# Pooled attention and a Mish feed-forward on one core: keys, queries and values laid out by the host, with a new order of work

## Chip, cores, metric

One core of a Trainium2 chip. The metric is the device time of one execution in microseconds (us). TensorE is PE (its weight loads PEld), VectorE DVE, ScalarE ACT, GpSimd POOL; SyncE (SP) issues the DMAs.

## What is computed

The reference, cut to what matters (B, H, S, D = 4, 8, 1152, 64; float32):

```
q_pool = q.reshape(B, H, S // 2, 2, D).mean(axis=3)
scores = q_pool @ k.T / sqrt(D);  scores -= scores.max(-1)
attn = exp(scores);  attn /= attn.sum(-1) + 1e-9
x = (attn @ v) as 2304 tokens of 512
h = x @ w_in;  g = h * tanh(softplus(h));  out = g @ w_out        # 512 -> 2048 -> 512
```

## The kernel before

**Attention** runs in 32 steps i. A pair p = i // 2 is two heads of one batch; a step is one half (288) of the pair's 576 pooled queries. The 1152 keys are nine chunks c of 128. Scores have keys on the partitions, and the two heads side by side (128 x 2 x 288). The functions of a step, with engine:

- QK(i, c) (L200, PE) writes the scores of one chunk to PSUM; two buffers of it exist (pool psS). CP(i, c) (L215, ACT) copies them into T3, which has one half for even and one for odd steps; MX(i, c) (L218, DVE) folds them into a running maximum rmax, in place.
- MT (L228, PE) transposes rmax, TMAX (L235, DVE) reduces it, MB and MBb (L240, L247, PE) spread the maxima again into PSUM.
- SUB(i, g) (L253, DVE) subtracts them from one of four groups of chunks (2, 2, 2 and 3), in place in T3; EXP(i, g) (L258, ACT) follows.
- ADD(i, 0 to 4) (L262, POOL) sums the exponentials over the chunks into acc, of which one buffer exists. PV(i, c) (L272, PE) multiplies them with the values, PVE (L286, ACT) takes the product out of PSUM.
- FIN0 (L293, PE) sums acc over the partitions; FLN, FEX (ACT), FE (DVE), FU (POOL) and FX (DVE, L332) divide and write the columns of xT.

**Queries and keys** come as they lie in memory. For each pair, load_q (L90) and load_k (L99) issue two DMAs each and load_v (L113) one; QP (L122, POOL, DVE for pair 0) adds neighbouring queries; TG(p, 0 to 3) (L139, PE) makes nine 128 x 128 transposes of keys and six 96 x 96 of queries in PSUM, and TGc (L153, ACT) copies them in five pieces to kT and qT. For pair 0, first() (L164) does this ahead of everything, behind 52 idle transposes (L174) on PE.

**The order** is written out by hand: STEP gives each function of a step a due time for even and for odd steps, in units of one step from the step's own start, PAIR those of a pair (unit: one step, pair p counted from 2p), CONV0 those of the first weights' conversion, XE and XL those of the split of the first columns of xT. All entries are sorted by due time and issued so; every engine, and the DMA queue of SP, then works in that order.

**Feed-forward.** Weights and x are split in a high and a low fp32r part; conv(n, 0 to 5) (L437) splits the weights (piece n: ACT, three operations on DVE, ACT, POOL), split_h, split_l and split_x split xT. H_ (L500) and O_ (L533) make three products each on PE, in five blocks of the 2048 features over nine groups of 256 tokens. The first blocks begin while step 31 ends; the entries of the list END set that seam.

Of the kernel before, what the change touches and what calls it, by code (L numbers as in the profile page):

```python
# [22 lines left out]
def tile_pooled_attention_then_mish_ffn(ctx: ExitStack, tc: tile.TileContext, q, k, v, moe_w_in, moe_w_out, out):  # L23
    nc = tc.nc
    B, H, S, D = q.shape
# [41 lines left out]
    if True:  # L67
# [30 lines left out]

        def load_k(p):  # L99
            if p >= B * NP:  # L100
                return
            b, hp = divmod(p, NP)
            kn = pre.tile([P, NC, 2, D], F32, tag="kn", name=f"kn{p}")
            for j in range(2):
                o = kn[:, :, j] if p else T3[:, 1, j].rearrange("p a b -> p (a b)").rearrange("p (c d) -> p c d", d=D)
                sp.dma_start(out=o, in_=k[b, 2 * hp + j].rearrange("(p c) d -> p c d", c=NC))
                if p == 0:
                    (act.copy if j else dve.tensor_copy)(kn[:, :, j], o)
            raw[p][0] = kn
# [3 lines left out]
        def load_v(p):  # L113
            if p >= B * NP:
                return
            b, hp = divmod(p, NP)
# [1 line left out]
            sp.dma_start(out=vs[p], in_=v[b, 2 * hp:2 * hp + 2].rearrange("h (p c) d -> p h c d", c=NC))

        prepped = {}  # L120

        def QP(p):  # L122

            x = raw[p][1].rearrange("p j n m -> p n j m")
            qp = pre.tile([QB, 6, 2, D], F32, tag="qp", name=f"qp{p}")
            (pool if p else dve).tensor_tensor(qp, x[:, :, :, 0:D], x[:, :, :, D:2 * D], ALU.add)
            prepped[p] = qp.rearrange("p n j d -> p n (j d)")
# [8 lines left out]
        def kblock(p, c):
            return raw[p][0][:, c].rearrange("p j d -> p (j d)")

        def TG(p, g):  # L139

            if p not in qk:
                qk_tiles(p)
            x = ps1.tile([P, 512], F32, tag="x", name=f"xt{p}_{g}")
            a = 0
            for n in {0: range(0, 4), 1: range(4, 8), 2: (8,), 3: ()}[g]:
                pe.transpose(x[:, a:a + P], kblock(p, n), ident)
                a += P
            for n in {2: range(0, 3), 3: range(3, 6)}.get(g, ()):
                pe.transpose(x[:, a:a + QB], prepped[p][:, n], ident[0:QB, 0:QB])
                a += QB  # L150
            xt[p, g] = x

        def TGc(p, g):  # L153
            kT, qT = qk[p]
            x = xt.pop((p, g))
            if g < 2:
                act.copy(kT[:, 4 * g:4 * g + 4], x.rearrange("p (n m) -> p n m", m=P))
            elif g == 2:
                act.copy(kT[:, 8], x[:, 0:P])
                act.copy(qT[:, 0:HQ], x[:, P:P + HQ])  # L160
            else:
                act.copy(qT[:, HQ:SQ], x[:, 0:HQ])

        def first():  # L164

            load_q(0)
            load_k(0)
            load_w(0)
            load_w(1)
            QP(0)  # L170
# [4 lines left out]
            qk_tiles(0)  # L175
            kT, qT = qk[0]
            t = psS.tile([P, 2, 512], F32, tag="S", name="xq0")
            for n in range(6):
                pe.transpose(t[:, n // 3, n % 3 * QB:(n % 3 + 1) * QB], prepped[0][:, n], ident[0:QB, 0:QB])
            act.copy(qT[:, 0:HQ], t[:, 0, 0:HQ])  # L180
            dve.tensor_copy(qT[:, HQ:SQ], t[:, 1, 0:HQ])
            x = psS.tile([P, 8, P], F32, tag="S", name="xk0")
            for n in range(8):
                pe.transpose(x[:, n], kblock(0, n), ident)
            act.copy(kT[:, 0:4], x[:, 0:4])
            dve.tensor_copy(kT[:, 4:8], x[:, 4:8])
            x = ps1.tile([P, 512], F32, tag="x", name="xk0_2")
            pe.transpose(x[:, 0:P], kblock(0, 8), ident)
            act.copy(kT[:, 8], x[:, 0:P])
            load_q(1)  # L190
            load_k(1)
# [147 lines left out]
        LQ, LK = -3.4, -2.2  # L339
        STEP = [  # L340
            (QK, 0, -0.5640, -0.5584),
            (CP, 0, -0.4042, -0.4268),
            (QK, 1, -0.3837, -0.4118),
            (QK, 2, -0.3395, -0.3676),
            (MX, 1, -0.3197, -0.2976),
            (MX, 2, -0.2628, -0.2408),
            (CP, 1, -0.2498, -0.3491),
            (CP, 2, -0.2033, -0.1585),
            (QK, 3, -0.1849, -0.2352),
            (QK, 4, -0.1407, -0.1056),  # L350
            (MX, 3, -0.1181, -0.1833),
            (MX, 4, -0.0612, -0.0387),
            (CP, 3, -0.0587, -0.1195),
            (QK, 5, 0.0172, -0.0614),
            (CP, 4, 0.0823, 0.0864),
            (MX, 5, 0.0835, 0.1060),
            (CP, 5, 0.1429, 0.1655),
            (QK, 6, 0.1527, 0.1835),
            (QK, 7, 0.1969, 0.2277),
            (MX, 6, 0.2282, 0.2507),  # L360
            (MX, 7, 0.2850, 0.3076),
            (CP, 6, 0.2876, 0.3102),
            (CP, 7, 0.3445, 0.3722),
            (QK, 8, 0.3974, 0.3918),
# [9 lines left out]
            (SUB, 2, 1.1559, 1.1334),
            (EXP, 1, 1.2264, 1.2039),
            (PV, 0, 1.3117, 1.2407),
            (ADD, 0, 1.3313, 1.3504),
            (PV, 2, 1.3481, 1.4854),
            (SUB, 3, 1.3575, 1.3349),
            (EXP, 2, 1.4746, 1.4124),  # L380
            (PV, 1, 1.4797, 1.3173),
            (PV, 3, 1.5200, 1.3537),
            (ADD, 1, 1.5913, 1.6104),
            (EXP, 3, 1.6349, 1.6900),
            (PV, 5, 1.7675, 2.1034),
            (ADD, 2, 1.7928, 1.8231),
            (PV, 8, 1.9331, 2.1397),
            (PV, 4, 1.9734, 1.8085),
            (ADD, 3, 1.9942, 2.0245),
            (PV, 7, 2.0687, 2.0670),  # L390
            (ADD, 4, 2.1024, 2.1328),
            (PV, 6, 2.1090, 2.0267),
            (PVE, 2.1820, 2.2046),
            (FIN0, 2.2809, 2.2714),
            (FLN, 2.3836, 2.4113),
            (FEX, 2.4924, 2.4490),
            (FE, 2.5303, 2.5472),
# [3 lines left out]
        PAIR = [
            (QP, -1.7894),
            (TG, 1, -1.2869),
            (TGc, 1, -1.1948),
            (TG, 2, -1.1438),
            (TGc, 2, -1.0804),
            (TG, 0, -1.0176),
            (TGc, 0, -0.9498),
            (TG, 3, -0.0969),
            (TGc, 3, 0.0605),  # L410
# [217 lines left out]
        plan = []  # L628
        for fn, *a, t0, t1 in STEP:
            t = t0, t1  # L630
            for i in range(NS):
                if (i, fn) in GONE:
                    continue
# [65 lines left out]
```

## Time and profile before

| | us |
|---|---|
| median of 3 runs (879.56 to 880.87) | 880.58 |
| profiled execution, its own time | 881.09 |
| its span, first to last instruction | 878.9 |
| PE, DVE, ACT, POOL busy in the span | 856.1, 601.9, 536.2, 455.2 |

The mean granted clock of TensorE is 0.988 of full speed. Some 2.2 us of the execution's time lie outside the span. Busy times of PE hold waits inside a pipelined group of matmuls, so 97% of the span is not PE at its peak. A timeline row gives start, duration, engine, line, operation, output <- input, shape and count; in brackets the idle time ahead of it and who ended it. A row that merges two operations (x2) runs from the start of the first to the end of the second.

### The profile page before, as it was taken

The page shows a single profiled execution, that of the slowest core. Times are in us where ns is not written, and L with a number is a line of the kernel's source. Part 1 is how long each engine was busy: PE and PEld are TensorE (multiplying, and loading weights), DVE is VectorE, ACT ScalarE, POOL GpSimd, SP SyncE. Part 2 cuts the span into 40 slices and gives each one's busy share as a digit, 9 for nine tenths or more (in the row PEclk, how much of TensorE's full clock was granted, in tenths as well). Part 3 has the DMA queues.
Part 4 walks back from the last instruction along what each step waited for, and adds up shares of the span by engine and source line. Part 5 has one row for each costly group of instructions (what it writes and reads, how often), then busy time and mean ns, then how long its engine had stood idle before and what let it go on. Part 6 is the DMA issues. An engine that isn't in the chain of part 4 may idle for free. (4 is left out here: it accounts for less than half of the span.)

```text
span 878.9 us, 14807 instructions
## 1 busy us (share of the span) xinstructions
PE 856.1 (97%) x5668; PEld 601.2 (68%) x5668; DVE 601.9 (68%) x813; ACT 536.2 (61%) x995; POOL 455.2 (52%) x267
## 2 busy tenths in 40 slices
PE   6799999999999999999989999999999999999997
PEld 4455555555555555555547889999889999999996
DVE  5889999999999999999988743443545344422222
ACT  4688889888898888988875563333333333322221
POOL 1489899999999999999896510110111011100000
PEclk9699999999999999999999999999999999999999
DMA  6413233122332222320200220110221011001112
GB/s 180 131 29 81 55 82 81 38 72 58 79 82 49 61 70 66 81 55 29 76 1 3 71 72 25 48 48 25 73 70 51 25 49 49 25 15 42 41 48 72
DMA packets 75111, 50.76 MB, mean 58 GB/s; under 512 B 37409, under 2 KB 68641, under 8 KB 75041
## 3 DMA queue, kind: packets, MB, share of 16 engines
q1 hardware_dynamic: 75040, 49.82, 20.2%
q8 instruction: 45, 0.74, 0.3%
q14 instruction: 26, 0.20, 0.1%
HBM read 45.09 MB, written 4.72 MB: 57 GB/s over the span
## 5 line engine op out<-in xcount | busy, mean ns | idle before, releaser
L524 DVE TENSOR_TENSOR gl<-g,gh 128x256 fp32r<-128x256 f32 x144 | 65.3, 453 | 225.3 <-ACT gh L519 199.0
L216 ACT COPY T<-s 128x576 f32<-128x576 f32 x288 | 180.9, 641 | 52.2 <-DVE rmax L223 46.1
L514 ACT ACTIVATE g<-h 128x256 f32<-128x256 f32 x144 | 55.4, 385 | 245.3 <-PE h L509 245.3
L206 PE MATMUL s<-qT,kT 64*128 64x288 f32 x1152 | 195.8, 449 | 8.4 <-ACT T L216 7.2
L256 DVE TENSOR_TENSOR T<-T,Mb 128x1152 f32<-128x1152 f32 (+1 forms) x128 | 191.2, 1495 | 1.4 <-PE Mb L250 1.4
L465 POOL TENSOR_TENSOR wl<-wt,wh 128x512 fp32r<-128x512 f32 x32 | 42.2, 1318 | 263.8 <-ACT wh L462 219.9
L278 PE MATMUL pv<-T,vn 128*64 128x288 f32 x1152 | 175.0, 422 | 2.5 <-ACT pvs L289 2.5
L223 DVE TENSOR_TENSOR rmax<-s,rmax 128x576 f32<-128x576 f32 x224 | 168.9, 754 | 10.9 <-PE s L206 0.9
L268 POOL TENSOR_TENSOR acc<-acc,T 128x1152 f32<-128x1152 f32 x64 | 168.8, 2638 | 8.7 <-POOL acc L268 6.0
L260 ACT ACTIVATE T<-T 128x1152 f32<-128x1152 f32 (+1 forms) x128 | 164.5, 1285 | 7.2 <-DVE T L256 7.2
L509 PE MATMUL h<-xh,wh 128*128 128x256 f32 x576 | 162.1, 281 | 0.0
L509 PE MATMUL h<-xh,wl 128*128 128x256 f32 x576 | 161.8, 281 | 0.0
L509 PE MATMUL h<-xl,wh 128*128 128x256 f32 x576 | 161.6, 281 | 0.0
L206 PEld LDWEIGHTS s<-qT,kT 64*128 64x128 f32 x1152 | 90.4, 188 | 92.5 <-ACT T L216 74.7
L278 PEld LDWEIGHTS pv<-T,vn 128*64 128x64 f32 x1152 | 72.4, 137 | 71.4 <-issue 28.0
L509 PEld LDWEIGHTS h<-xh,wh 128*128 128x128 f32 x576 | 108.7, 189 | 8.2 <-issue 1.3
L509 PEld LDWEIGHTS h<-xl,wh 128*128 128x128 f32 x576 | 108.8, 189 | 6.0
L509 PEld LDWEIGHTS h<-xh,wl 128*128 128x128 f32 x576 | 109.2, 190 | 0.0
L266 POOL TENSOR_TENSOR acc<-T 128x1152 f32<-128x1152 f32 x32 | 84.7, 2648 | 32.0 <-PE Sb L300 13.8
L542 PE MATMUL o<-wh,gh 128*128 128x512 f32 x146 | 57.8, 396 | 1.0 <-ACT xT L554 1.0
L542 PE MATMUL o<-wl,gh 128*128 128x512 f32 x146 | 57.6, 394 | 0.0
L542 PE MATMUL o<-wh,gl 128*128 128x512 f32 x146 | 57.3, 392 | 0.0
(384 smaller groups left out, 1106.3 us busy)
## 6 DMA issues: line engine op xcount, KB each, us to landing
qn<-in_q_dram SPq DMA_DIRECT2D x32, 288.0 KB, 3.9
vn<-in_v_dram SPq DMA_DIRECT2D x16, 576.0 KB, 5.0
kn<-in_k_dram SPq DMA_DIRECT2D x30, 288.0 KB, 4.1
ri<-in_moe_w_in_dram SPq DMA_DIRECT2D x64, 128.0 KB, 2.2
ro<-in_moe_w_out_dram SPq DMA_DIRECT2D x16, 512.0 KB, 3.4
out_dram<-xT SPq DMA_DIRECT2D x18, 256.0 KB, 2.6
T<-in_k_dram SPq DMA_DIRECT2D x2, 288.0 KB, 5.0
```

The costliest lines, as they stand in the source:

```text
L206: pe.matmul(s[:, j, 0:HQ], kT[64 * j:64 * j + 64, c], qT[64 * j:64 * j + 64, hf * HQ:(hf + 1) * HQ], start=True, stop=True,)
L216: act.copy(T3[:, i % 2, c], ss[i, c])
L223: dve.tensor_tensor(r, ss[i, c], T3[:, i % 2, 0] if c == 1 else r, ALU.max)
L256: dve.tensor_tensor(x, x, Mbs[i][:, :, 0:HQ].unsqueeze(1).to_broadcast([P, w, 2, HQ]), ALU.subtract)
L260: act.activation(x, x, AF.Exp, scale=0.0625)
L266: pool.tensor_tensor(accs[i], t[:, 0:2], t[:, 2:4], ALU.add)
L268: pool.tensor_tensor(accs[i], accs[i], t[:, 2 * n + 2:2 * n + 4], ALU.add)
L278: pe.matmul(pvs[i][64 * j:64 * j + 64, 0:HQ], vn[:, j, c, :], T3[:, i % 2, c, j], start=(pvn[i] == 1), stop=(pvn[i] == NC),)
L509: pe.matmul(h[:, 0:UT], a, b, start=(m == 0), stop=(m == len(seq) - 1))
L514: act.activation(g, hs[bu, f], AF.Mish)
L524: dve.tensor_tensor(gl, ch.pop((bu, f)), f32(gs[bu, f][0]), ALU.subtract)
L542: pe.matmul(os_[bu][t], x, y, start=(first and m == 0), stop=(last and m == 2))
```

## The change

The host hands over q, k and v in other layouts: for each pair q as (head and feature 128, half 2, even or odd query 2, 288), k as (head and feature 128, chunk 9, 128), v as (128, head 2, chunk 9, 64). So kT is loaded by one DMA, QP adds straight into qT, and TG, TGc and the pair-0 transposes and copies are gone. All due times are new. A list FILL holds 281 entries with due times of their own for the first four steps or so; it has conv of the first four weight pieces and all early loads in it. Core of the diff:

```
-            qn = pre.tile([QB, 2, 6, P], F32, tag="qn", name=f"qn{p}")
-            for j in range(2):
-                sp.dma_start(out=qn[:, j], in_=q[b, 2 * hp + j].rearrange(...))
+            if p not in raw:
+                raw[p] = pre.tile([P, 2, 2, HQ], F32, tag="qn", name=f"qn{p}")
+            for a, z in halves or ((0, 2),):
+                sp.dma_start(out=raw[p][:, a:z], in_=q[p][:, a:z])
...
+            for a, z in parts or ((0, NC),):
+                sp.dma_start(out=qk[p][0][:, a:z], in_=k[p][:, a:z])
...
-        def TG(p, g):
-        def TGc(p, g):
...
+        def QP(p):
+            x = raw[p]
+            pool.tensor_tensor(qk[p][1], x[:, :, 0], x[:, :, 1], ALU.add)
+        def QH(n):
+            (pool if n in QHP else dve).tensor_tensor(qk[0][1][:, n], raw[0][:, n, 0], raw[0][:, n, 1], ALU.add)
...
         def first():
-            load_q(0)
...
+            qk_tiles(0)
             if NWARM:
...
-        LQ, LK = -3.4, -2.2
+        LQ, LK, QHP = -2.342, -2.2, (1,)
         STEP = [
...
-            (MX, 8, 0.4747, 0.4973),
-            (TMAX, 0.5963, 0.6255),
-            (SUB, 0, 0.8666, 0.7871),
-            (SUB, 1, 1.0113, 0.9887),
-            (FU, 2.5518, 2.5327),
-            (FX, 2.6512, 2.5981),
+            (MX, 8, 0.3645, 0.3594),
+            (TMAX, 0.6411, 0.6326),
+            (SUB, 0, 0.8146, 0.9207),
+            (SUB, 1, 1.0418, 0.7726),
+            (FU, 2.6678, 2.4802),
+            (FX, 2.9627, 2.7399),
...
-            (QP, -1.7894),
-            (TG, 1, -1.2869),
...
+            (QP, -0.8418),
...
+        FILL = [
+            (-0.700, load_q, 0, (0, 1)),
+            (-0.586, load_k, 0, (0, 2)),
+            (-0.536, load_k, 0, (2, 5)),
+            (-0.460, load_k, 0, (5, 9)),
+            (-0.429, QH, 0),
+            (-0.378, QK, 0, 0),
+            (-0.359, load_w, 0),
...
+            (1.536, conv, 1, 3),
+            (1.597, load_w, 3),
+            (1.798, load_q, 2),
...
-        XE = [5.349, 7.349, 9.349, ...
-        XL = 1.892
+        XE = [6.123, 8.123, 10.123, ...
+        XL = 0.055
...
-        for n, t in enumerate(CONV0):
-            plan += [(t[m], conv, n, m) for m in range(6)]
```

In the new order DVE does this in two steps of the steady part (steps in brackets, 0 being the even one; from the due times, not shown in the diff above): MX4[0] MX5[0] SUB2[-1] MX6[0] MX7[0] MX8[0] SUB3[-1] FE[-2] MX1[1] TMAX[0] MX2[1] MX3[1] SUB0[0] MX4[1] FX[-2] MX5[1] SUB1[0] MX6[1] MX7[1] SUB2[0] MX8[1] SUB3[0] FE[-1] MX1[2] TMAX[1] MX2[2] FX[-1] SUB1[1] MX3[2] SUB0[1].

## Rows read from the trace of the kernel before

**Rows 1.** Windows: stretch, us, busy PE, PEld, DVE, ACT, POOL (instructions), PE clock, DMA share, GB/s.
```profile
100.00:150.00 50.00, 50.00 (x351) 25.84 (x349) 47.32 (x56) 44.33 (x70) 46.64 (x26) 1.00 0.25 60
...
600.00:700.00 100.00, 100.00 (x643) 90.44 (x642) 47.91 (x87) 33.25 (x89) 12.69 (x10) 1.00 0.15 50
```

**Rows 2.** Timeline of DVE: TMAX of steps 4, 30 and 31.
```profile
85.70 0.83 DVE L237 TENSOR_REDUCE m<-mt 128x5 f32<-128x640 f32 x1 [0.43 <-PE mt L232]
...
439.73 0.83 DVE L237 TENSOR_REDUCE m<-mt 128x5 f32<-128x640 f32 x1 [0.43 <-PE mt L232]
...
453.71 0.82 DVE L237 TENSOR_REDUCE m<-mt 128x5 f32<-128x640 f32 x1
```

**Rows 3.** Timeline of DVE within one pair of steady steps.
```profile
212.14 1.61 DVE L223 TENSOR_TENSOR rmax<-s,rmax 128x576 f32<-128x576 f32 x2
213.67 1.34 DVE L256 TENSOR_TENSOR T<-T,Mb 128x1152 f32<-128x1152 f32 x1
214.94 0.75 DVE L223 TENSOR_TENSOR rmax<-s,rmax 128x576 f32<-128x576 f32 x1
215.60 1.34 DVE L256 TENSOR_TENSOR T<-T,Mb 128x1152 f32<-128x1152 f32 x1
...
218.40 1.95 DVE L256 TENSOR_TENSOR T<-T,Mb 128x1728 f32<-128x1728 f32 x1
220.26 0.75 DVE L223 TENSOR_TENSOR rmax<-s,rmax 128x576 f32<-128x576 f32 x1
...
221.87 0.83 DVE L237 TENSOR_REDUCE m<-mt 128x5 f32<-128x640 f32 x1 [0.43 <-PE mt L232]
222.61 0.45 DVE L334 SCALAR_TENSOR_TENSOR xT<-Sb,pvs 128x288 f32<-128x288 f32 x1
```

**Rows 4.** Waits of DVE, 100 to 450 us: total us, times, longest.
```profile
DVE m L237 <- PE mt L232: 5.6, 13, 0.4
DVE rmax L223 <- ACT T L216: 2.7, 13, 0.2
DVE xT L334 <- POOL pvs L330: 1.9, 12, 0.2
```

**Rows 5.** Timeline, PE weight loads and DVE: from TMAX to SUB.
```profile
223.01 0.41 PEld L245 LDWEIGHTS Mb<-identr,m 128*128 128x128 f32 x4 [0.38 <-DVE m L237]
...
455.01 0.45 PEld L245 LDWEIGHTS Mb<-identr,m 128*128 128x128 f32 x4
...
455.95 1.35 DVE L256 TENSOR_TENSOR T<-T,Mb 128x1152 f32<-128x1152 f32 x1 [1.42 <-PE Mb L250]
```

**Rows 6.** Groups by line, 100 to 450 us, and one wait of POOL: busy us, mean ns.
```profile
L146 PE MATMUL xt<-identr,kn 128*128 128x128 f32 x108 | 19.0, 285 | 0.0
...
L157 ACT COPY kT<-xt 128x512 f32<-128x512 f32 x24 | 13.7, 572 | 0.0
...
L270 POOL TENSOR_TENSOR acc<-acc,T 128x576 f32<-128x576 f32 x26 | 36.8, 1414 | 2.0
...
L126 POOL TENSOR_TENSOR qp<-qn 96x768 f32<-96x768 f32 x12 | 22.1, 1839 | 0.0
...
POOL acc L266 <- PE Sb L300: 10.8, 13, 1.5
```

**Rows 7.** Timeline of the start: warm-up, first QK, first MX, an operation of conv.
```profile
1.62 5.74 PE L174 MATMUL warm<-identr 128*128 128x128 f32 x52 [1.62 <-DVE cst L73]
...
10.57 2.25 PE L206 MATMUL s<-qT,kT 64*128 64x288 f32 x16 [0.57 <-ACT kT L185]
...
12.04 0.76 DVE L223 TENSOR_TENSOR rmax<-s,T 128x576 f32<-128x576 f32 x1 [0.80 <-ACT T L216]
...
14.03 0.69 DVE L449 SCALAR_TENSOR_TENSOR wt<-ri,wt 128x512 int32<-128x512 int32 x1
```

**Rows 8.** The page's DMA issues: KB each, us to landing.
```profile
qn<-in_q_dram SPq DMA_DIRECT2D x32, 288.0 KB, 3.9
```

**Rows 9.** Timeline of ACT at the seam: the second EXP of step 31.
```profile
461.11 1.16 ACT L260 ACTIVATE T<-T 128x1152 f32<-128x1152 f32 x1 [2.61 <-DVE T L256]
```

More of the change, by code (lines that the diff above doesn't have):

```diff
@@ L24, in tile_pooled_attention_then_mish_ffn @@
     nc = tc.nc
-    B, H, S, D = q.shape
+    B, H, S, D = SHAPE
     SQ = S // 2
@@ L88, in tile_pooled_attention_then_mish_ffn, with load_q, load_k @@
         raw, qk = {}, {}
-        def load_q(p):
+        def load_q(p, *halves):
             if p >= B * NP:
                 return
-            b, hp = divmod(p, NP)
-            qn = pre.tile([QB, 2, 6, P], F32, tag="qn", name=f"qn{p}")
-            for j in range(2):
-                sp.dma_start(out=qn[:, j], in_=q[b, 2 * hp + j].rearrange("(n p r) d -> p n (r d)", p=QB, r=2))
-            raw[p] = [None, qn]
-        def load_k(p):
+            if p not in raw:
+                raw[p] = pre.tile([P, 2, 2, HQ], F32, tag="qn", name=f"qn{p}")
+            for a, z in halves or ((0, 2),):
+                sp.dma_start(out=raw[p][:, a:z], in_=q[p][:, a:z])
+        def load_k(p, *parts):
             if p >= B * NP:
                 return
[L102 to L109, printed above, removed]
+            if p not in qk:
+                qk_tiles(p)
+            for a, z in parts or ((0, NC),):
+                sp.dma_start(out=qk[p][0][:, a:z], in_=k[p][:, a:z])
         vs = {}
@@ L115, in load_v @@
                 return
-            b, hp = divmod(p, NP)
             vs[p] = p2.tile([P, 2, NC, D], F32, tag="vn", name=f"vn{p}")
[L118 to L127, printed above, removed]
+            sp.dma_start(out=vs[p], in_=v[p])
         def qk_tiles(p):
-            qT = pqk.tile([P, SQ], F32, tag="qT", name=f"qT{p}")
+            qT = pqk.tile([P, 2, HQ], F32, tag="qT", name=f"qT{p}")
             kT = pqk.tile([P, NC, P], F32, tag="kT", name=f"kT{p}")
             qk[p] = (kT, qT)
-        xt = {}
-        def kblock(p, c):
-            return raw[p][0][:, c].rearrange("p j d -> p (j d)")
-        def TG(p, g):
[L141 to L151, printed above, removed]
-        def TGc(p, g):
[L154 to L162, printed above, removed]
-        def first():
-            load_q(0)
[L167 to L170, printed above, removed]
+        def QP(p):
[3 more added lines that the diff above has]
+            (pool if n in QHP else dve).tensor_tensor(qk[0][1][:, n], raw[0][:, n, 0], raw[0][:, n, 1], ALU.add)
+        def first():
+            qk_tiles(0)
             if NWARM:
@@ L174, in first @@
                     pe.transpose(x[:, n % 4], identr, identr)
[L175 to L191, printed above, removed]
         rmaxs, Mbs, pvs, pvn, accs = {}, {}, {}, {}, {}
@@ L220, in MX @@
             if c == 1:
-                rmaxs[i] = p2.tile([P, 2, HQ], F32, tag="rmax", name=f"rmax{i}")
-            r = rmaxs[i]
+                rmaxs[i, 1] = p2.tile([P, 2, HQ], F32, tag="rmax", name=f"rmax{i}")
+            r = rmaxs[i, 1]
             dve.tensor_tensor(r, ss[i, c], T3[:, i % 2, 0] if c == 1 else r, ALU.max)
@@ L337, in FX @@
             )
-        LQ, LK = -3.4, -2.2
+        LQ, LK, QHP = -2.342, -2.2, (1,)
         STEP = [
[L341 to L364, printed above, removed]
-            (MX, 8, 0.4747, 0.4973),
-            (CP, 8, 0.5342, 0.5567),
-            (MT, 0.5357, 0.5638),
-            (TMAX, 0.5963, 0.6255),
-            (MB, 0.6761, 0.7042),
-            (MBb, 0.7532, 0.7486),
-            (SUB, 0, 0.8666, 0.7871),
-            (EXP, 0, 0.9701, 0.9804),
-            (SUB, 1, 1.0113, 0.9887),
[L374 to L397, printed above, removed]
-            (FU, 2.5518, 2.5327),
-            (FX, 2.6512, 2.5981),
@@ new lines, in tile_pooled_attention_then_mish_ffn @@
+            (QK, 0, -0.5640, -0.5668),
+            (CP, 0, -0.4998, -0.5027),
+            (QK, 1, -0.4954, -0.5204),
+            (MX, 1, -0.4185, -0.4100),
+            (QK, 2, -0.3821, -0.3716),
+            (CP, 1, -0.3186, -0.4627),
+            (MX, 2, -0.3112, -0.3027),
+            (CP, 2, -0.2495, -0.2410),
+            (QK, 3, -0.2433, -0.3263),
+            (CP, 3, -0.1871, -0.1748),
+            (MX, 3, -0.1304, -0.2365),
+            (QK, 4, -0.1125, -0.1665),
+            (QK, 5, -0.0673, -0.1213),
@@ new lines, in tile_pooled_attention_then_mish_ffn @@
+            (CP, 4, -0.0386, 0.0034),
+            (CP, 5, 0.0014, 0.0581),
+            (MX, 4, 0.0177, -0.0884),
+            (MX, 5, 0.0839, -0.0093),
+            (QK, 6, 0.1007, 0.0840),
+            (QK, 7, 0.1463, 0.1292),
+            (CP, 6, 0.1692, 0.2306),
+            (MX, 6, 0.2320, 0.1451),
+            (QK, 8, 0.2944, 0.2972),
+            (MX, 7, 0.2982, 0.2113),
+            (CP, 7, 0.3599, 0.3008),
+            (MX, 8, 0.3645, 0.3594),
+            (CP, 8, 0.4262, 0.4512),
+            (MT, 0.5746, 0.5641),
@@ new lines, in tile_pooled_attention_then_mish_ffn @@
+            (TMAX, 0.6411, 0.6326),
+            (MB, 0.7200, 0.6995),
+            (MBb, 0.7653, 0.7449),
+            (SUB, 0, 0.8146, 0.9207),
+            (EXP, 0, 0.9214, 1.0414),
+            (SUB, 1, 1.0418, 0.7726),
+            (EXP, 1, 1.1486, 0.8794),
+            (PV, 1, 1.1740, 1.3884),
+            (PV, 3, 1.2525, 1.3472),
+            (SUB, 2, 1.2624, 1.1350),
+            (ADD, 0, 1.2725, 1.2524),
+            (PV, 2, 1.3500, 1.5243),
+            (EXP, 2, 1.3692, 1.2419),
+            (PV, 0, 1.3912, 1.2323),
@@ new lines, in tile_pooled_attention_then_mish_ffn @@
+            (SUB, 3, 1.4105, 1.4156),
+            (ADD, 1, 1.5383, 1.4601),
+            (EXP, 3, 1.5634, 1.5773),
+            (ADD, 2, 1.7460, 1.7259),
+            (PV, 5, 1.8015, 2.0020),
+            (PV, 4, 1.8427, 1.7847),
+            (ADD, 3, 1.9537, 1.9336),
+            (PV, 6, 1.9775, 2.0392),
+            (PV, 7, 2.0187, 1.9235),
+            (PV, 8, 2.0560, 1.9647),
+            (ADD, 4, 2.0660, 2.0459),
+            (PVE, 2.1468, 2.0981),
+            (FIN0, 2.1911, 2.2152),
+            (FLN, 2.3238, 2.2714),
@@ L400, in tile_pooled_attention_then_mish_ffn @@
+            (FEX, 2.4662, 2.3408),
+            (FE, 2.5586, 2.5535),
+            (FU, 2.6678, 2.4802),
+            (FX, 2.9627, 2.7399),
         ]
         PAIR = [
-            (QP, -1.7894),
-            (TG, 1, -1.2869),
[L404 to L410, printed above, removed]
+            (QP, -0.8418),
             (load_q, LQ),
@@ L455, in conv @@
                 )
-                if n + 2 not in (4, 5):
+                if n > 3:
                     load_w(n + 2)
@@ L576, in tile_pooled_attention_then_mish_ffn @@
         CV3 = [0, 1, 2, 3, 4, 5]
-        LW, REUSE = -0.5, -0.438
+        LW, REUSE = -0.5, -0.544
         XD, ED = (2, 3), ()
@@ L626, in reuse_rest @@
             open_pool("x3", 1)
-        plan = []
+        plan = [e for e in FILL]
+        gone = set(GONE) | {e[1:] for e in FILL}
         for fn, *a, t0, t1 in STEP:
@@ L631, in tile_pooled_attention_then_mish_ffn @@
             for i in range(NS):
[L632 removed]
+                if (i, fn) in GONE or (fn, i, *a) in gone:
                     continue
@@ L637, in tile_pooled_attention_then_mish_ffn @@
         for fn, *a, t in PAIR:
-            first_p = 2 if fn in (load_q, load_k) else 0 if fn is load_v else 1
-            plan += [(2 * p + t, fn, p, *a) for p in range(first_p, B * NP)]
-        CONV0 = [
-            (-0.26, -0.17, -0.16, -0.13, -0.05, -0.04),
-            (-0.02, 0.07, 0.09, 0.10, 0.20, 0.21),
-            (0.35, 0.40, 0.47, 0.49, 0.55, 0.56),
-            (0.60, 0.66, 0.67, 0.78, 0.85, 0.86),
-        ]
-        for n, t in enumerate(CONV0):
-            plan += [(t[m], conv, n, m) for m in range(6)]
+            plan += [(2 * p + t, fn, p, *a) for p in range(1, B * NP) if (fn, p, *a) not in gone]
         plan += [(NS + LW, load_w, n) for n in (4, 5)]
@@ L669, in tile_pooled_attention_then_mish_ffn @@
         close("x3", "w4", "x2", "ag", "x1", "x0", "w0", "wraw", "psH", "ps1")
+SHAPE = (4, 8, 1152, 64)
 _INS = ["q", "k", "v", "moe_w_in", "moe_w_out"]
@@ L684 @@
     arrays, args = {}, []
+    b, h, s, d = SHAPE
+    laid = dict(inputs)
+    laid["q"] = inputs["q"].reshape(b * h // 2, 2, 2, s // 4, 2, d).transpose(0, 1, 5, 2, 4, 3).reshape(b * h // 2, 2 * d, 2, 2, s // 4)
+    laid["k"] = inputs["k"].reshape(b * h // 2, 2, 128, s // 128, d).transpose(0, 1, 4, 3, 2).reshape(b * h // 2, 2 * d, s // 128, 128)
+    laid["v"] = inputs["v"].reshape(b * h // 2, 2, 128, s // 128, d).transpose(0, 2, 1, 3, 4)
     for name in _INS:
-        a = _np.ascontiguousarray(inputs[name])
+        a = _np.ascontiguousarray(laid[name])
         if a.dtype == _np.float64:
```

279 lines of the change are left out of this document (275 added, 4 removed).

## The prediction

> **What bounds the kernel now.** I read the windows first. From 600 us on PE is busy all the time and nothing else comes near it [rows 1]: that is the feed-forward, which the change leaves as it is. In the attention stretch PE also shows 100%, but its weight loads fill only half of it, while DVE is busy for 47.3 of 50 us, POOL for 46.6 and ACT for 44.3 [rows 1]. So attention is a loop in which DVE has almost no room left. Its length comes from the timeline of DVE: TMAX of step 4 starts at 85.70, of step 30 at 439.73, of step 31 at 453.71 [rows 2]. That is 354.03 us for 26 steps, 13.62 us a step, 27.23 a pair of steps. The waits of DVE say what its idle time is: in a pair 0.43 us for the transposes of MT, 0.21 for a CP and 0.16 for FU [rows 4], the totals divided by the 13 pairs in the window.
>
> The price of a DVE operation depends on its neighbour [rows 3]. An MX that is followed by something else holds DVE for 0.66 us (214.94 to 215.60), an MX followed by another MX of the same maximum for 0.86 (the row with two lasts 1.61, its second 0.75). A SUB costs 1.27 (213.67 to 214.94), the long one 1.86 (218.40 to 220.26), TMAX 0.74; FX, lasting 0.45, about 0.4, and FE I take as the same (estimates: the duration less the overlap). In a pair: 16 MX 10.6, 6 short SUB 7.6, 2 long 3.7, 2 TMAX 1.5, 4 FE or FX 1.6, together 25.0. The old list has 6 places with MX behind MX, 0.20 more each: 26.2. With the 0.8 of named waits that is 27.0 of 27.23, so the sum explains the period.
>
> **Part 1, what is removed in the loop.** Per pair PE loses 15 transposes (those of keys 19.0 us in 12 pairs [rows 6], 1.6 a pair; the queries less) and ACT five copies (two at 0.57 [rows 6], three smaller: 1.1 to 2.9 us). Neither engine is the bound, so by themselves they bring nothing. QP on POOL becomes 576 elements on 128 partitions instead of 768 on 96: 1.41 by the nearest row of that shape, 1.84 if it stays as it was [rows 6]. I take 1.41. What the removal buys is freedom to reorder, because no transpose has to be fitted between QK and PV on PE any more.
>
> **Part 2, the new order in the loop.** The new DVE sequence has 5 places with MX behind MX, not 6: 26.0 us. The three waits: before, only FE lies between the last MX of an even step and its TMAX; now a long SUB, FE and an MX do, some 2.9 us, against 0.86 from the end of that MX to TMAX (221.01 to 221.87 [rows 3]), so the 0.43 goes. MX1 of the odd step now comes 0.09 steps (1.2 us) after its CP0 by the due times, which last about 0.05; the 0.21 goes. FX comes 0.26 to 0.30 steps (3.4 us or more) after FU, where FU was just ahead; the 0.16 goes. What is late next: from TMAX to the first SUB that needs its maxima the path over MB and MBb takes 1.14 us (221.87 [rows 3] to 223.01 [rows 5]) and 0.94 (455.01 to 455.95 [rows 5]), 2.08 in all. In the odd step TMAX, MX2 and FX fill only 0.74 + 0.66 + 0.4 = 1.8 of that before SUB1: a wait of 0.3. In the even step TMAX, two MX behind each other and SUB0 give 2.3, no wait. So a pair takes 26.0 + 0.3 = 26.3, and I take 26.4 for small mismatches, 13.2 a step. Bounds: 26.0 with no wait at all, 27.0 if as much is waited as before. I stay near the lower end because each old wait has a reason to go. Over the 27 steps from TMAX of step 4 to that of step 31 the loop then gives 27 x (13.62 - 13.2) = **11.3 us** (0 waits: 16; 27.0 a pair: 3).
>
> Beside it POOL is busy 46.64 / 50 x 27.23 = 25.4 a pair [rows 1], 25.0 with the smaller QP: it fits in 26.4 with 1.4 to spare. split_l moves nearly two steps earlier, 0.7 us or so into a gap of POOL. load_k is due 2.2 steps ahead, behind the last QK that reads the same buffer (2.7 ahead) and 1.6 steps, 21 us, before the first that needs it; a load lands 3.9 us after its issue [rows 8]. Loads cost nothing there, one DMA for two. If the cover went, 4 us a pair would show.
>
> **Part 3, the start.** Before, QK of pair 0 waits for loads, QP, transposes and copies until 10.57, and the first MX starts at 12.04 [rows 7]. Now the first half of q and two chunks of k are issued first; landing 3.9 to 5 us after an issue at some 0.7 to 1.2 us, they are there before the warm-up on PE, which is unchanged and ends at 1.62 + 5.74 = 7.36 [rows 7]. QK then starts at 7.4 and MX 1.47 later as before, at 8.8. From there the list has 63 us of DVE work up to TMAX of step 4: 41 MX 27.1 and 7 neighbours 1.4, 12 short SUB 15.2, 4 long 7.4, 4 TMAX 3.0, 5 FE or FX 2.0, and 12 operations of conv at 0.69 [rows 7], 0.6 after the overlap, 7. The old start had the same work and took 85.70 - 12.04 = 73.7, so 10.7 us were waits, in steps run at steady due times with conv pushed in between. The new list is made for these steps; its waits lie between 0 and 10.7. I take 4: the loop's share before (0.8 of 27.2) would give 2, and low clock on PE may add to that. TMAX of step 4 comes at 8.8 + 63 + 4 = 75.8: **9.9 us** earlier (3 to 14). SP works in order: load_w(3) waits for conv(1, 3), due 0.06 steps ahead of it, and load_q(2) stands behind; QP(2) needs that 1.28 steps (17 us) later, so a short hold is covered.
>
> **Part 4, the seam.** In step 31 SUB1 now precedes SUB0, and the two operations of split_x on DVE come between them. EXP0 is still first on ACT, so it starts where EXP1 did, at 461.11 [rows 9] counted as now, and EXP1, and behind it PVE, which frees the PSUM of PV for step 31, come later by one EXP, 1.16 less overlap: **1.1 us lost** (0 to 2). Feed-forward: 0.
>
> **Sum.** 881.09 - 11.3 - 9.9 + 1.1 = 861.0 for the profiled execution; the median is 0.5 below it: **860.5 us**.
>
> **A rule against it.** The rows show an operation of DVE starting before the one ahead has ended (215.60 against 214.94 + 0.75), unless it reads that one's result [rows 3]. [...]
>
> **Rivals.**
> - *The loop does not get shorter*: DVE's operations need their whole durations, 27.4 a pair, in any order, or another wait of 0.9 us a pair takes the place of the old ones. Then only start and seam are left, 880.58 - 9.9 + 1.1 = 872. For it: the 0.3 of the odd step is already such a wait. Against: the overlap in rows 3. Chance 0.12. [...]
> - *Half-way*: DVE waits on PE at several places, 26.8 to 27.0 a pair, or the start loses 8: 864 to 869. The weight loads' share leaves PE room, but the due times of MT, MB and SUB are tight. Chance 0.20.
> - *POOL becomes the bound, slower than before.* acc has one buffer, so ADD0 waits for FIN0 of the step before, which stands on PE behind QK that may wait itself. It cost 10.8 us in 13 pairs, at most 1.5 at a time [rows 6]. If both steps of a pair paid 1.5 and QP stayed at 1.84, POOL would need 25.4 + 3.0 = 28.4 a pair, 14.2 a step: 27 x 0.58 = 15.7 more, 880.58 + 15.7 - 9.9 + 1.1 = 887. It decides from 26.4 a pair on, and makes the kernel slower than before from 27.9. Against: the waits would have to reach their longest value everywhere. Chance 0.07.
> - *Gains eaten to nothing*, within 0.2%: 0.04.
>
> That the change doesn't do what it says is no rival: the transposes and copies are deleted in the diff. The forecast itself has 0.57: 26.0 to 26.7 a pair with 0 to 7 us of waits in the start, 852 to 865.
>
> **Numbers.** 0.2% is 1.8 us, about what a measurement of this kernel can tell from no change. The range runs from 852 (no waits in loop or start, seam as now: 861 - 5 - 4 = 852) to 872, the first rival; it leaves out the last two rivals and half of the first. Faster 0.88, same 0.04, slower 0.08.
>
> **What would show it.** TMAX of step 4 at 75.8 (73 to 80); TMAX to TMAX 26.4 a pair; no wait of DVE for FU or CP, but one of 0.3 on MBb in odd steps; first QK at 7.4, right behind the warm-up; step 31's first EXP 3 to 4 us later against its TMAX; feed-forward of the same length. It is wrong if POOL waits for nothing while DVE idles, or if QK waits for loads.

## The result, and the profile after

The changed kernel takes **859.63 us** (median of 4 runs, 859.24 to 860.8) against 880.35 of the kernel before on the same chip: a ratio of 0.977 (95% interval 0.975 to 0.979). The forecast was 860.5. Its profiled execution took 859.45, 857.6 of it span. The total fits closely, but that is partly luck: the loop gave 3.6 us more than forecast and the start 3.1 less, and these two errors cancel.

**The loop.** The timeline of DVE has TMAX of steps 4, 6 and 31 here (compare [rows 2]):

```profile
78.93 0.82 DVE L176 TENSOR_REDUCE m<-mt 128x5 f32<-128x640 f32 x1
...
105.10 0.82 DVE L176 TENSOR_REDUCE m<-mt 128x5 f32<-128x640 f32 x1
...
432.06 0.83 DVE L176 TENSOR_REDUCE m<-mt 128x5 f32<-128x640 f32 x1 [0.48 <-PE mt L171]
```

From step 4 to step 31 that is 353.13 us for 27 steps, 13.08 a step, 26.17 a pair (105.10 - 78.93). Before it was 368.01. The loop gave 14.9 us.

The windows of one steady stretch, to be laid beside [rows 1] (stretch; busy us of PE, PEld, DVE, ACT, POOL with instructions; PE clock; DMA share; GB/s):

```profile
100.00:150.00 50.00, 48.92 (x334) 24.07 (x332) 48.85 (x58) 43.81 (x63) 47.92 (x27) 1.00 0.20 72
```

DVE went from 47.3 to 48.9 of 50 us. The waits of DVE from 100 to 430 us, which before were the three of [rows 4], are an empty list now. The timeline of DVE around TMAX of an odd step shows what stands in their place:

```profile
219.26 0.75 DVE L162 TENSOR_TENSOR rmax<-s,rmax 128x576 f32<-128x576 f32 x1
219.93 1.94 DVE L195 TENSOR_TENSOR T<-T,Mb 128x1728 f32<-128x1728 f32 x1
221.79 0.46 DVE L254 SCALAR_TENSOR_TENSOR Sb<-Sb,rs 128x288 f32<-128x288 f32 x1
222.16 0.75 DVE L162 TENSOR_TENSOR rmax<-s,T 128x576 f32<-128x576 f32 x1
222.82 0.81 DVE L176 TENSOR_REDUCE m<-mt 128x5 f32<-128x640 f32 x1
223.56 0.75 DVE L162 TENSOR_TENSOR rmax<-s,rmax 128x576 f32<-128x576 f32 x1
224.22 0.45 DVE L273 SCALAR_TENSOR_TENSOR xT<-Sb,pvs 128x288 f32<-128x288 f32 x1
224.59 1.35 DVE L195 TENSOR_TENSOR T<-T,Mb 128x1152 f32<-128x1152 f32 x1
```

No row has a bracket: DVE waits for nothing here. Between the last MX of the step (219.26) and its TMAX stand a long SUB, FE and an MX of the next step. In the even step before, where the wait of 0.43 was, the same three do (the SUB starts at 206.81):

```profile
208.67 0.46 DVE L254 SCALAR_TENSOR_TENSOR Sb<-Sb,rs 128x288 f32<-128x288 f32 x1
209.15 0.76 DVE L162 TENSOR_TENSOR rmax<-s,T 128x576 f32<-128x576 f32 x1
209.82 0.81 DVE L176 TENSOR_REDUCE m<-mt 128x5 f32<-128x640 f32 x1
```

Between TMAX of the odd step and the first SUB with its maxima (224.59) stand an MX and FX, and that was just enough. PE's weight loads say why:

```profile
223.69 0.41 PEld L184 LDWEIGHTS Mb<-identr,m 128*128 128x128 f32 x4 [0.77 <-DVE m L176]
```

MB starts 0.06 us after the end of TMAX (222.82 + 0.81). In [rows 5] it started 0.31 after it, at 223.01. PE stood at two QK then, as its timeline in the kernel before shows:

```profile
221.79 1.30 PE L206 MATMUL s<-qT,kT 64*128 64x288 f32 x8
```

In the even step of the new order two QK stand there as well, and MB starts 0.23 after the end of TMAX (210.86 against 209.82 + 0.81).

**The start.** TMAX of step 4 comes at 78.93, 6.8 us earlier than before. The first MX starts at 9.51, and from there to 78.93 DVE waits for 0.25 us only. The time is lost elsewhere. DVE's operations of conv, which took 0.69 [rows 7], take here (four of the twelve, timeline of DVE):

```profile
15.90 0.68 DVE L384 SCALAR_TENSOR_TENSOR wt<-ri,wt 128x512 int32<-128x512 int32 x1
...
26.39 1.69 DVE L378 TENSOR_SCALAR wt<-wt 128x512 int32<-128x512 int32 x1
...
33.86 1.81 DVE L384 SCALAR_TENSOR_TENSOR wt<-ri,wt 128x512 int32<-128x512 int32 x1
...
47.69 2.75 DVE L384 SCALAR_TENSOR_TENSOR wt<-ro,wt 128x512 int32<-128x512 int32 x1
```

And POOL in the same stretch:

```profile
25.15 2.65 POOL L205 TENSOR_TENSOR acc<-T 128x1152 f32<-128x1152 f32 x1 [2.77 <-ACT T L199]
...
32.51 2.62 POOL L207 TENSOR_TENSOR acc<-acc,T 128x1152 f32<-128x1152 f32 x1 [1.94 <-ACT T L199]
...
47.26 2.63 POOL L207 TENSOR_TENSOR acc<-acc,T 128x1152 f32<-128x1152 f32 x1 [1.08 <-ACT T L199]
```

An operation that falls into an ADD ends 0.3 to 0.6 us after that ADD: 26.39 + 1.69 = 28.08 against 27.80, 33.86 + 1.81 = 35.67 against 35.13, 47.69 + 2.75 = 50.44 against 49.89. It does its work when POOL has finished, as far as these ends show. The twelve take 13.3 us in all, where 7.2 would do (four at 0.42, eight at 0.69).

**The seam.** From TMAX of step 31 to the end of the span it was 878.9 - 453.71 = 425.19 us, now 857.6 - 432.06 = 425.54. ACT, and PE right after it:

```profile
438.74 2.22 ACT L199 ACTIVATE T<-T 128x1152 f32<-128x1152 f32 x2 [4.65 <-DVE T L195]
440.86 0.39 ACT L228 ACTIVATE pvs<-pv 128x288 f32<-128x288 f32 x1
```
```profile
441.31 3.57 PE L217 MATMUL pv<-T,vn 128*64 128x288 f32 x16 [3.02 <-ACT pvs L228]
```

SUB1 goes first and SUB0 comes behind split_x, but EXP0 is first on ACT. So both EXP start late, PVE stands behind them, and PE idles for 3.02 us. PE's granted clock is 0.68 from 441 to 446 us, behind that idle time. But the kernel before had the same wait, of 2.51, so that only 0.35 is lost by the change:

```profile
462.62 3.67 PE L278 MATMUL pv<-T,vn 128*64 128x288 f32 x16 [2.51 <-ACT pvs L289]
```

**What held.** QP takes 1.42 us (L120, 12 in 17.0 us), as taken. POOL waits for FIN0 once in the loop, 1.1 us, not 13 times [rows 6].

### The profile page after: what moved, and what is told of

It reads as the page before. It is cut to its first block, busy times and chain, and to the rows that moved or that the text cites. A ratio compares the mean times of both kernels' runs of the same rounds, so it can differ in the third digit from the quotient of the medians.

```text
span 857.6 us, 14083 instructions
## 1 busy us (share of the span) xinstructions
PE 826.5 (96%) x5428; PEld 574.8 (67%) x5428; DVE 598.5 (70%) x810; ACT 513.2 (60%) x916; POOL 451.5 (53%) x268
```

## The experiments

### The layouts without the new order

The changed kernel with all due times of the kernel before (STEP, QP, LQ, XE, XL, CONV0), and FILL cut to the early loads:

```
-        LQ, LK, QHP = -2.342, -2.2, (1,)
+        LQ, LK, QHP = -3.4, -2.2, (1,)
...
-            (MX, 8, 0.3645, 0.3594),
+            (MX, 8, 0.4747, 0.4973),
-            (TMAX, 0.6411, 0.6326),
+            (TMAX, 0.5963, 0.6255),
...
-            (QP, -0.8418),
+            (QP, -1.7894),
```

> The host's layouts, so no transposes and copies of keys and queries, but every due time of before (steps, pairs, first weights, split of the first columns); the loads and additions of pair 0 stand ahead of everything, as there. Theory (DVE's order sets the loop, PE and ACT had room): a pair of steps stays at 26.9 to 27.3 us, and only the start and nothing else gains 1 to 4 us: 874 to 879 us. Rival (less work on PE and ACT shortens the loop by itself): a pair at 26.6 or less and 862 to 868 us.

Measured: 877.4 us (877.16 to 877.95), a ratio of 0.997 (0.996 to 0.999). TMAX of steps 4 and 6, and the waits of DVE from 100 to 430 us (total, times, longest):

```profile
81.27 0.83 DVE L176 TENSOR_REDUCE m<-mt 128x5 f32<-128x640 f32 x1 [0.43 <-PE mt L171]
...
108.50 0.83 DVE L176 TENSOR_REDUCE m<-mt 128x5 f32<-128x640 f32 x1 [0.43 <-PE mt L171]
```
```profile
DVE m L176 <- PE mt L171: 5.1, 12, 0.4
DVE rmax L162 <- ACT T L155: 2.5, 12, 0.2
DVE xT L273 <- POOL pvs L269: 1.8, 11, 0.2
```

A pair takes 27.23 as before, with the same three waits, as the theory had it. Taking 15 transposes and five copies a pair away gives nothing in the loop by itself; the gain there comes only with the new order. The start gains 4.4 us by the layouts alone (81.27 against 85.70 [rows 2]).

### The transposes and copies put back under the new order

From pair 3 on PE transposes keys that lie in memory already, and ACT copies the products to a buffer that nobody reads, so nothing of the computation changes:

```
+        def TG(p, g):
+            x = ps1.tile([P, 512], F32, tag="x", ...)
+                pe.transpose(x[:, a:a + w], kT[0:w, n], ident[0:w, 0:w])
+        def TGc(p, g):
+                act.copy(d, x)
         PAIR = [
+            (TG, 1, -1.0300), (TGc, 1, -0.9700), (TG, 2, -0.9500), (TGc, 2, -0.8800),
+            (TG, 0, -0.2400), (TGc, 0, -0.1700), (TG, 3, -0.0969), (TGc, 3, 0.0605),
```

> The changed kernel with the removed work put back beside it: from pair 3 on the same 15 transposes on PE a pair (of keys already there) and the same five copies on ACT, into a tile that nobody reads, at places where their PSUM buffer is free in the new order. Theory (PE and ACT have room; the order of DVE is what counts): a pair at 26.2 to 26.7 us, 859 to 866 us. Rival (the gain of the loop comes from the work taken off PE and ACT): 27 us or more a pair, 870 us or more.

Measured: 890.5 us (890.0 to 891.0), ratio 1.012 (1.009 to 1.015): **slower than the kernel before**, a pair at 28.6. The theory (PE and ACT have room for them) fell. Three more runs split it: PE's part alone, two of its four groups alone, and ACT's part alone (copies of the same shapes, but read from SBUF).

> The changed kernel, but from pair 3 on PE makes the fifteen transposes of each pair again (of keys that lie in memory already; nobody reads what they write), without ACT's copies of them. Theory (PE works in order, so a QK that stands behind a transpose which waits for its PSUM buffer comes late, and MX with it): most of the 31 us that transposes and copies cost together, a pair at 27.5 to 28.6, 876 to 891. Rival (it is ACT, which has 3 us a pair free and gets 2.9 of copies): a pair at 26.2 to 26.6, 859.5 to 865.

> The run with PE's transposes back, but only two of the four groups of each pair (four of 128 x 128 and three of 96 x 96, at -0.24 and -0.10, some 1.0 us of PE in the row of the run with all four). Theory (PE's order has no slack left where QK feeds MX, so PE's added time goes into the period one for one): a pair 0.9 to 1.1 us longer than 26.17, that is 27.1 to 27.3, 870 to 875 in all. Rival (one place decides, the QK behind the groups at -1.03 and -0.95, where DVE waits 1.33 us): a pair at 26.2 to 26.6, 859.5 to 865.

> The changed kernel, but from pair 3 on ACT makes the five copies of each pair again (from keys in SBUF, read by nobody), without PE's transposes. Theory (the loss of the run with both is PE's): a pair at 26.2 to 26.6, 859.5 to 865. Rival (ACT is the engine that has no room: 43.8 of 50 us busy, 22.9 a pair of 26.2, and 2.9 more leave 0.4): DVE waits for CP at many MX, a pair at 27.2 to 28.6, 872 to 891.

| put back | time, us | ratio (interval) | a pair, us |
|---|---|---|---|
| nothing | 859.63 | 0.977 (0.975 to 0.979) | 26.17 |
| ACT's copies | 868.9 | 0.987 (0.985 to 0.988) | 26.92 |
| two groups on PE | 873.24 | 0.992 (0.990 to 0.994) | 27.22 |
| four groups on PE | 889.73 | 1.010 (1.009 to 1.012) | 28.47 |
| both | 890.5 | 1.012 (1.009 to 1.015) | 28.6 |

The waits of DVE from 100 to 400 us, with four groups on PE:

```profile
DVE rmax L162 <- PE s L145: 13.3, 10, 1.3
DVE rmax L162 <- ACT T L155: 10.3, 32, 0.4
```

And a stretch of PE in that run, with two of the four groups:

```profile
197.86 0.66 PE L347 MATMUL xt<-identr,kT 128*128 128x128 f32 x4
198.45 1.19 PE L217 MATMUL pv<-T,vn 128*64 128x288 f32 x8
199.57 0.58 PE L347 MATMUL xt<-identr,kT 128*128 128x128 f32 x4
```

From its start to that of the next row each group holds PE: the first for 0.59 us (198.45 - 197.86), and so read all four hold it for 0.59, 0.51, 0.59 and 0.40 us, 2.09 in all, and the pair grows by 2.30. The two groups of the smaller run hold it for 0.99, and the pair grows by 1.05. So **time added to PE at these places goes into the period about one for one**, though PE's weight loads fill only half of it (24.07 of 50 us). The waits of DVE above say the same: 23.6 us in the 10.5 pairs of the window, 2.24 a pair. The rival of one decisive place fell. ACT's run fell between its theory (859.5 to 865) and its rival (872 to 891): the copies cost 0.75 a pair alone and almost nothing beside the transposes.

That is a matter of place, not of PE's capacity, which the kernel before shows. One of its groups of transposes:

```profile
223.50 0.60 PE L146 MATMUL xt<-identr,kn 128*128 128x128 f32 x4
```

It holds PE for 0.53 us, up to the next row at 224.03. The other groups of that pair, read in the same way at 212.38, 225.41 and 227.16, hold it for 0.39, 0.51 and 0.59, which makes 2.02 in all. The pair takes 27.23 with them, so all the rest of PE's work fits into 25.2, less than the 26.17 of the new loop.

This answers what the removal is worth in the loop. Alone, nothing (27.23 and 27.23). The order alone, with transposes at these places, loses. Together they give 1.06 a pair. It wasn't tried whether other places for the transposes would cost less; the one PSUM buffer that they can use is taken from FIN0 to FX.

### The list of the first four steps taken away

FILL keeps only the early loads and QH; the first steps run at the due times of STEP, and conv at those of the kernel before:

```
         FILL = [
...
-            (-0.378, QK, 0, 0),
-            (-0.333, QK, 0, 1),
-            (-0.314, CP, 0, 0),
...
+        plan += [(t[m], conv, n, m) for n, t in enumerate(CONV0) for m in range(6)]
```

> The changed kernel without the list for the first steps: new order of the period from step 0 on, first weights and loads at the times of before. Theory (the list takes the waits out of the start): a pair at 26.2 us as in the changed kernel, TMAX of step 4 at 81 to 85 us instead of 78.9, whole time 862 to 866 us. Rival (the start is earlier only because the first MX is, the list itself gives nothing): TMAX of step 4 at 78 to 80 us and 859 to 861 us.

Measured: 859.49 us (859.11 to 859.86), ratio 0.976 (0.974 to 0.979), no different from the changed kernel. TMAX of step 4 comes at 79.97, 1.0 later than with the list, not 2 to 6: both numbers are the rival's. The windows of 16 to 40 us, first without the list, then with it:

```profile
16.00:24.00 8.00, 5.74 (x23) 2.58 (x23) 6.69 (x11) 4.94 (x10) 1.30 (x2) 0.58 0.50 177
24.00:32.00 8.00, 5.61 (x24) 3.06 (x26) 7.76 (x11) 4.55 (x7) 3.88 (x3) 0.71 0.00 0
32.00:40.00 8.00, 7.88 (x38) 3.47 (x35) 5.85 (x7) 4.89 (x7) 5.27 (x2) 0.64 0.46 141
```
```profile
16.00:24.00 8.00, 5.98 (x39) 3.05 (x39) 7.57 (x10) 6.69 (x11) 2.64 (x2) 1.00 0.19 68
24.00:32.00 8.00, 6.30 (x41) 2.75 (x39) 8.00 (x9) 6.24 (x8) 5.33 (x2) 1.00 0.00 0
32.00:40.00 8.00, 6.83 (x47) 3.14 (x46) 8.00 (x9) 5.84 (x9) 7.06 (x4) 1.00 0.40 149
```

With the list DVE is all but full and PE's granted clock stays at 1.00. Without it the clock is 0.58 to 0.71 and DVE waits some 5 us, but conv is done on DVE by 28.4 us, before POOL's first ADD at 33.7, and its operations keep their short times (0.42 to 0.71). The twelve take 7.5 us in sum there and 13.3 with the list. The list trades waits for held operations.

### POOL's ADD left out of the first steps

ADD(i, 1 to 4) are not issued for i = 0, 1 and 2, so the denominators of these steps miss terms.

```
+            if i < 3 and n > 0:
+                return
```

> The changed kernel with ADD 1 to 4 of steps 0, 1 and 2 left out, so that POOL is idle beside most of the first weights' conversion (the sums of these steps are then those of four chunks, folded no further). Theory (DVE's operations of conv are held while POOL reads SBUF): the 12 operations, 13.3 us in sum in the changed kernel against 7.2 at their shortest durations, fall to 9 us or less, and TMAX of step 4 comes 3 to 6 us earlier, at 73 to 76 us. Rival (they are held by their own inputs, ACT's copy or the loads of the weights): the sum stays above 12 us and TMAX of step 4 within 1.5 us of 78.9.

Measured, in a single run: 856.35 us, TMAX of step 4 at 75.38, 3.55 earlier. The operation that took 2.75 us, and its neighbour that took 1.22:

```profile
46.80 0.67 DVE L386 SCALAR_TENSOR_TENSOR wt<-ro,wt 128x512 int32<-128x512 int32 x1
48.06 0.67 DVE L382 SCALAR_TENSOR_TENSOR wt<-ro,wt 128x512 int32<-128x512 int32 x1
```

The twelve sum to some 9.8 us, 3.55 less; the theory had put 9 or less. The four that stay long (1.69, 1.05, 0.78 and 1.40) each end 0.28 or 0.55 us after an operation of POOL that was left in (ADD0 or conv). So 3.55 of the 6 us are the price of the ADD left out, and the rest goes with other POOL work. The rival, with TMAX of step 4 within 1.5 us of 78.9, fell.

### All of conv ahead of the first ADD

```
-            (1.044, conv, 1, 1), ... (3.187, conv, 3, 5),
+            (0.330, conv, 1, 1), ... (0.900, conv, 3, 5),
-                r = wraw_p.tile([P, DM, 2], I32, tag="raw", ...)
+                r = pre.tile([P, DM, 2], I32, tag=f"raw{n}", ...) if n in (2, 3) else wraw_p.tile(...)
```

> The changed kernel, but all of conv of the first four weight pieces is issued before POOL's first ADD (the raw weights of pieces 2 and 3 get buffers of their own; their loads and load_k(1) come earlier). Theory (DVE's operations of conv are stretched only while POOL works): each at 0.42 to 0.69 us but those beside the QH, conv 5 of POOL; the twelve take 7 to 9 us instead of 13.3, TMAX(4) comes at 73 to 76 instead of 78.93, 854 to 857 in all. Rival (moving them ahead only puts off the MX that feed SUB, EXP and so POOL, whose ADD come later by the same time; POOL or ACT then sets the pace): TMAX(4) at 78 to 81, 858.5 to 862.

Measured: 860.25 us (859.6 to 862.24, the profiled execution being the longest of the five), ratio 0.977 (0.976 to 0.979). The operations are short now but for two (1.08 and 1.65), yet TMAX of step 4 comes at 80.14. From the first MX, which comes at 8.77 here, it is 71.4 us, against 69.4 in the changed kernel. DVE waits for 2.3 us at one place (37.5), for 1.1 at two more and for 5.9 in all, against 0.25, while the twelve operations save 4.8. POOL, in whose order conv's last operation now stands ahead of ADD, waits for it for 15.5 us against 12.3 in the changed kernel (up to 80 us: total, times, longest):

```profile
POOL wl L396 <- ACT wh L393: 15.5, 4, 7.0
```

POOL's first ADD starts at 32.2 instead of 25.15. PE's granted clock is 0.60 and 0.72 in the two windows from 20 to 40 us, and how much of the waits is due to that was not separated. Both numbers are the rival's: what DVE saves comes back as waits. No version that computes the whole result got the 6 us back.

### The seam: SUB0 ahead of SUB1 again

```
         END = {
+            (SUB, NS - 1, 0): -0.23,
```

> The changed kernel, but SUB(31, 0) is issued ahead of SUB(31, 1) as in the kernel before. Theory (the second EXP of step 31 sets the start of PVE and of the feed-forward, and it comes late because SUB1 goes first and SUB0 late): EXP0 starts at 3 us after TMAX(31) instead of 6.7 and PV starts 0.3 to 1.1 us earlier, 858.5 to 859.3 in all. Rival (EXP1, which is then second, ends as late as EXP0 now, since SUB1 is the one delayed; PE has other work there anyway): within 0.2 us of the changed kernel, 859.4 to 859.8.

Measured: **857.08 us** (856.78 to 857.86), ratio 0.974 (0.972 to 0.975), a larger gain than expected. Both SUB now stand ahead of split_x, which the kernel before had between them. ACT of this run:

```profile
435.50 2.43 ACT L199 ACTIVATE T<-T 128x1152 f32<-128x1152 f32 x2 [1.42 <-DVE T L195]
437.84 0.39 ACT L228 ACTIVATE pvs<-pv 128x288 f32<-128x288 f32 x1
```

PVE comes 3.0 us earlier, PE idles no more ahead of the 16 PV, and they take 2.16 us instead of 3.57, at granted clock 1.00. But the timelines show a new loss: gl, the low part of the Mish output, beside POOL's ADD of step 31.

```profile
444.98 1.82 DVE L738 TENSOR_TENSOR gl<-g,gh 128x256 fp32r<-128x256 f32 x1 [3.74 <-ACT gh L733]
...
446.72 2.92 DVE L738 TENSOR_TENSOR gl<-g,gh 128x256 fp32r<-128x256 f32 x1
```
```profile
443.87 2.65 POOL L205 TENSOR_TENSOR acc<-T 128x1152 f32<-128x1152 f32 x1 [2.97 <-PE Sb L239]
446.59 2.76 POOL L207 TENSOR_TENSOR acc<-acc,T 128x1152 f32<-128x1152 f32 x1
```

Each gl ends 0.28 us after the ADD it fell into (446.80 against 446.52, 449.64 against 449.35), the third after the next. PE then waits 0.60 at 452.99, for an operation of DVE that stands behind these gl, and 1.45 at 457.98, for a later gl.

### The ADD of step 31 on DVE

```
+            e = pool if i < NS - 1 else dve
-                pool.tensor_tensor(accs[i], accs[i], ...)
+                e.tensor_tensor(accs[i], accs[i], ...)
         END = {
+            (ADD, NS - 1, 0): 0.42, (ADD, NS - 1, 1): 0.43,
+            (ADD, NS - 1, 2): 0.53, (ADD, NS - 1, 3): 0.54, (ADD, NS - 1, 4): 0.55,
```

> The run with SUB(31, 0) ahead of SUB(31, 1), and besides the five ADD of step 31 go from POOL to DVE, with a buffer of their own for the sum: two of them ahead of the first gl, three behind it. Theory (gl, 0.43 us by itself, is held beside these ADD until POOL's operation ends, and takes 1.8, 2.9 and 2.7 us; PE then waits 0.6 and 1.45 us at 453.0 and 458.0): gl takes 0.4 to 1.0, the two waits of PE go, 854 to 856 in all. Rival (gl reads what ACT has just written and is slow for that reason, or the ADD on DVE put the gl and LX off by as much as the hold did): 857 to 859.

Measured: **853.2 us** (852.99 to 854.22), ratio 0.970 (0.968 to 0.971), below the expected range. DVE:

```profile
442.66 1.36 DVE L208 TENSOR_TENSOR acc<-acc,T 128x1152 f32<-128x1152 f32 x1
445.03 1.53 DVE L739 TENSOR_TENSOR gl<-g,gh 128x256 fp32r<-128x256 f32 x3 [1.01 <-ACT gh L734]
```

Three gl take 1.53 us, an ADD 1.36 instead of 2.76 on POOL. The windows of 432 to 460 us give PE's busy time in the changed kernel, in the run before this one and in this one:

```profile
432.00:460.00 28.00, 24.98 (x172) 18.99 (x171) 21.90 (x18) 14.99 (x29) 20.08 (x11) 0.94 0.00 1
```
```profile
432.00:460.00 28.00, 25.94 (x181) 19.38 (x180) 23.10 (x22) 16.40 (x33) 21.60 (x13) 1.00 0.02 4
```
```profile
432.00:460.00 28.00, 27.99 (x197) 21.76 (x196) 22.58 (x29) 17.26 (x35) 13.99 (x11) 1.00 0.07 20
```

From TMAX of step 31 to the end it is 425.54, 423.16 and 419.24 us. Of the last 3.9 us, 2.05 are these two waits and 1.0 is a later wait of O for the output's copy on ACT, which went as well; the rest was not traced.

### A shorter warm-up

On top of the last version, `NWARM = 44` instead of 52.

> The run with the ADD of step 31 on DVE, but with 44 instead of 52 idle transposes on PE ahead of the first QK. Theory (the first QK, at 8.0, waits for the end of the warm-up alone and not for data, so 8 transposes of some 0.12 us less give it back): first QK at 7.0 to 7.2, first MX at 8.5, TMAX(4) 0.8 to 1.0 us earlier, 852.2 to 852.5 in all. Rival (the keys are not there earlier, or PE's granted clock falls without them, or DVE's operations of conv, which ACT and the loads feed, just wait): TMAX(4) within 0.3 us of 78.96 or later, 853 to 855.

Measured: 852.56 us (852.35 to 853.96), ratio 0.970 (0.968 to 0.971), not to be told from 52. In the trace the first QK starts at 7.37 instead of 8.06, right behind the warm-up as the theory had it, and TMAX of step 4 at 78.35 instead of 78.96. But that the 8 transposes bring it is not shown. The same 52 transposes lasted 5.74 to 5.80 us in three traces and 6.34 to 6.66 in the nine others, and two traces of the new kernels with 52 have the first QK at 7.29 and 7.34. Why their time varies stays open.

## Why the prediction was right, point by point

- **Part 1** holds: the removal by itself is worth nothing in the loop (27.23 without the transposes). But the share of weight loads, from which a rival took that PE has room, is no measure of it: at the places tried the new loop takes on PE's added time almost whole.
- **Part 2** had the mechanism right: all three waits went, for the reasons given, and five MX stand behind an MX. The size was off by its new wait: "a wait of 0.3" before SUB1 in odd steps did not come. The 1.14 from TMAX to MB was read where MB stood behind two QK on PE, the second of which (221.79 + 1.30) outlasted TMAX; in the new order one QK stands there and MB starts 0.06 after the end of TMAX. From TMAX to that SUB it is 1.77 (222.82 to 224.59), what TMAX, MX2 and FX fill, so there is nothing to spare. A chain's price was taken with its neighbour's queue in it. A pair takes 26.17, the forecast's 26.0 without a wait and 0.17 of small gaps: 14.9 us instead of 11.3.
- **Part 3** was too high, 9.9 against 6.8. The first MX came 0.7 later than put (the warm-up's end). And the waits of 4 us were nearly absent, but "12 operations of conv at 0.69" cost 13.3 us and not 7: each was priced from one that ran while POOL stood still. The kernel before shows such stretched operations too (1.03 us at 17.90 and 1.24 at 23.73, where 0.42 would do). Of the 10.7 that the prediction called waits of the old start, its trace names 6.9. The 4 us of waits that did not come hide most of the 6 us of holding that did. And the list brought 1.0 of the 6.8: the layouts alone bring 4.4, and the new order of the steps with them 5.7. That split_l moves nearly two steps earlier was misread, as split_h moves too: it is 1.06 steps (5.349 + 1.892 against 6.123 + 0.055), and no term rests on it.
- **Part 4** put 1.1 lost and 0.35 were. EXP0 did stand behind a late SUB0; but PVE, 8.47 us behind TMAX of step 31 before, was only 0.33 later, since EXP0 and EXP1 now run back to back. That 2.5 us were to be had there was not seen; whether the kernel before would have gained them too was not run.
- **The rivals.** POOL did not become the bound: its waits for FIN0 nearly vanished, and it is busy for 47.9 of 50 us. The loop that doesn't get shorter did not come either. Its 27.4 a pair is the sum of the whole durations in [rows 3] (16 x 0.75 + 6 x 1.34 + 2 x 1.95 + 2 x 0.83 + 4 x 0.45); 26.17 is under it, and FX starts at 224.22 beside an MX that ends at 224.31. The Trainium skill, VectorE: DVE Perf Modes, The DRAIN you can't avoid, says that the next operation does not start until the pipe has emptied, and adds that one that is not held starts earlier; the trace agrees with the addition.
- **What would show it.** Right: QK behind the warm-up, no wait of DVE for FU or CP, step 31's first EXP 6.68 us behind its TMAX, 3.1 more than before. Wrong: TMAX of step 4 (78.93, within the range, not 75.8), and the wait on MBb.

Put together: 881.09 - 14.9 - 6.8 + 0.35 = 859.7, and the profiled execution took 859.45.

## What to carry to other kernels

Price an operation by its neighbours on all engines that share something with it, not only by the one ahead on its own: an operation of DVE that works in SBUF alone, beside a long POOL operation, costs that operation's remainder, and moving the POOL work to DVE can be cheaper than leaving it there. Room on an engine that works in order is shown by adding work at a place, not by a busy share, and it is shown for that place alone. When a removal gives nothing alone, look at which order it allows, and test order and removal apart.
